# Decayed linear attention and feed-forward: two heads per step on 128 partitions, with zero-padded queries and a 128x128 state

**Chip, cores, metric.** One core of one Trainium2 chip. The metric is the device time of one execution in microseconds (us); medians of several executions are given, with the lowest and highest in brackets.

## The reference

Attention with a decay per head, for B=4 batches, H=8 heads, S=768 tokens, D=64; its result, laid out as x (3072 x 512), goes through a feed-forward part 512 -> 2048 -> 512.

```python
# per head; lam is a scalar per head, near 0.97..0.99
for each block of tokens:
    intra = (qb @ kb.T * Dmask) @ vb              # Dmask[i,j] = lam**(i-j) for i >= j, else 0
    inter = (qb * lam_pow) @ kv_state             # lam_pow[i] = lam**(i+1)
    out[block] = intra + inter
    kv_state = lam_block * kv_state + (kb * rev_pow).T @ vb
...
h = x @ w_in
g = where(h >= 1, h, where(h <= -1, 0, (h + 1)**2 / 4))
return g @ w_out
```

The block length may be chosen freely; both kernels use 128 tokens, so 6 blocks a head.

## The kernel before

q, k and v of two heads are loaded together, q and k scaled on ScalarE into `qkdd` (128 tokens on the partitions, 6 blocks, 4 x 64 columns) and transposed on TensorE. From there each head works by itself on 64 rows or 64 columns of the array.

```python
BLK, GRP = 128, 3
for b in range(B):
    for hp in range(H // 2):
        # ... DMAs of q (L125), k (L128), v (L131); scalings (L137, L140) on ScalarE ...
        qTp = work.tile([128, NCH, 128], BF16, ...)      # two heads: rows 0-63 and 64-127
        kTp = work.tile([128, NCH, 128], BF16, ...)
        # transposes in groups of 4 and 2 into ptr (L152), copies ptr -> qTp, kTp on VectorE (L156)
        for hi in range(2):                              # each head by itself
            ps = hi * 64
            qT, kT = qTp[ps:ps + 64, :, :], kTp[ps:ps + 64, :, :]
            kdd = qkdd[:, :, 2 * D + ps:2 * D + ps + 64]
            for g in range(NG):
                for bi in range(GRP):                    # array form 64*128
                    nc.tensor.matmul(psc[:, bi, :], lhsT=kT[:, blk, :], rhs=qT[:, blk, :], ...)   # L172
                nc.vector.scalar_tensor_tensor(out=sc, in0=psc, scalar=laminvblk[h][:, 0:1],
                                               in1=_bc(causalT, 128, GRP, 128), ...)               # L175
                for bi in range(GRP):
                    nc.tensor.matmul(po[:, bi, :], lhsT=v_bf[:, blk, ps:ps + 64],
                                     rhs=sc[:, bi, :], ...)                        # L183, 128*64
                    if kv is not None:
                        nc.tensor.matmul(po[:, bi, :], lhsT=kv, rhs=qT[:, blk, :], ...)  # L188, 64*64
                    nc.tensor.matmul(pkv[ps:ps + 64, :], lhsT=kdd[:, blk, :],
                                     rhs=v_bf[:, blk, ps:ps + 64], ...)            # L192, 128*64
                    # kv_new = kv * lam**128 + pkv on VectorE (L199 for the first, L202)
                nc.scalar.copy(out=xT[pstart:pstart + 64, ko, ...], in_=po)        # L209
# ... then the feed-forward part, L226 to L252: not touched by the change ...
```

"Array form 64*128" stands for a matmul that contracts over 64 rows and uses 128 columns of the array. The tiles in the profiles: `ptr` holds transposes of q and k, `psc` the scores and `sc` the masked scores, `po` the output of attention, `pkv` what a block adds to the state `kv`; in the feed-forward part, `ph` is the first product and `py` the second.

## Time and profile before

| | before |
|---|---|
| time, median of 4 runs | 387.87 us (387.73 to 388.43) |
| span of the profiled run | 386.0 us |
| end of the last xT copy (end of attention) | 207.1 us |
| rest of the span (feed-forward) | 178.9 us |
| one pair of heads, steady | 10.60 us |

Two rows of the page matter later: the 40 slices of the span (9.65 us each), in tenths busy, and the row of TensorE's granted clock.

### The profile page before, as it was taken

Reading aid. Unit: us, or ns where it says so; the run is one execution under the profiler, and the core shown is the slowest. Engines: PE = TensorE matmul, PEld = TensorE weight load, DVE = VectorE, ACT = ScalarE, POOL = GpSimd, SP = SyncE. Lnnn points to the kernel's source line nnn. Section 1 sums busy time; section 2 is a strip of 40 time slices with the busy share of each in tenths; the row PEclk is TensorE's granted clock in tenths of the full one; section 3 lists DMA queues with packets and bytes.
Section 4 is the critical chain, followed back from the end, with each engine's and each line's share of the span. In section 5 each row is a group of like instructions: output and inputs, shape, how many; then the busy total and the mean of one; then the engine's idle time right before and its main releaser. Section 6 shows DMA issues by size and latency. Waiting matters only on the chain.

```text
span 386.0 us, 5043 instructions
## 1 busy us (share of the span) xinstructions
PE 332.0 (86%) x1680; PEld 161.8 (42%) x1696; DVE 213.3 (55%) x621; ACT 200.9 (52%) x379; POOL 29.5 (8%) x43
## 2 busy tenths in 40 slices
PE   0023899999999999999989999999999999999995
PEld 0012455555555554555543444434434434434432
DVE  1112666666666666666645854834844843852850
ACT  7212333443434433334416966946946955955961
POOL 6000101111111111001100000000000000000000
PEclk9999999999999999999999999999999999999999
DMA  7999977676656655333300011011011011011001
GB/s 154 200 193 192 221 109 102 104 102 99 83 77 77 96 95 93 20 22 21 23 0 0 2 55 54 2 54 55 2 55 54 2 54 54 3 55 55 2 35 75
DMA packets 81482, 26.55 MB, mean 69 GB/s; under 512 B 75824, under 2 KB 77872, under 8 KB 81456
## 3 DMA queue, kind: packets, MB, share of 16 engines
q1 hardware_dynamic: 53776, 18.88, 21.2%
q0 software_dynamic: 27680, 7.34, 18.8%
q8 instruction: 13, 0.21, 0.2%
q14 instruction: 13, 0.11, 0.1%
HBM read 27.27 MB, written 6.29 MB: 87 GB/s over the span
## 4 chain that ended last, share of the span: by engine, by line
PE 60%; DVE 16%; ACT 10%; SPq 5%; issue 4%; DMA 3%; DVEq 0%; ACTq 0%
PE py L246 18%; PE po L183 10%; PE po L188 9%; PE psc L172 7%; PE ptr L152 6%; PE ph L226 6%; DVE a L240 5%; DVE gT L241 5%; ACT cc L235 4%; DMA qk_nat<-in_q_dram 3%; PE pkv L192 3%; DVE aa L238 3%; ACT xT L209 3%; SPq L128 3%; SPq L125 2%
## 5 line engine op out<-in xcount | busy, mean ns | idle before, releaser
L226 PE MATMUL ph<-xT,w_in_sb 128*128 128x512 bf16 x375 | 96.1, 389 | 1.3 <-DVE sc L175 0.2
L246 PE MATMUL py<-w_out_sb,gT 128*128 128x512 bf16 x377 | 92.9, 380 | 2.9 <-DVE gT L241 1.9
L235 ACT ACTIVATE cc<-ph,cm 128x512 bf16<-128x512 f32 x96 | 77.2, 804 | 0.0
L232 ACT ACTIVATE tt<-ph,chalf 128x512 bf16<-128x512 f32 x96 | 76.5, 797 | 1.2 <-PE ph L226 1.2
L209 ACT CAST xT<-po 64x384 bf16<-64x384 f32 x64 | 30.2, 472 | 81.8 <-PE po L188 81.5
L202 DVE SCALAR_TENSOR_TENSOR kv_new<-kv_new,lamblk,pkv 64x64 bf16<-64x64 bf16 x160 | 44.4, 277 | 30.1 <-PE pkv L192 23.2
L226 PEld LDWEIGHTS <-w_in_sb 128*128 128x128 bf16 x384 | 37.7, 98 | 50.7 <-issue 11.3
L246 PEld LDWEIGHTS <-gT 128*128 128x128 bf16 x384 | 35.7, 98 | 52.3 <-DVE gT L241 12.6
L152 PE MATMUL ptr<-ident,qkdd 128*128 128x128 bf16 x192 | 28.8, 307 | 32.3 <-ACT qkdd L137 27.2
L192 PE MATMUL pkv<-v_bf,qkdd 128*64 128x64 bf16 x192 | 49.3, 257 | 8.3 <-DVE kv_new L202 8.3
L238 DVE TENSOR_SCALAR aa<-tt 128x512 bf16<-128x512 bf16 x96 | 27.6, 288 | 51.6 <-ACT tt L232 51.6
L183 PE MATMUL po<-sc,v_bf 128*64 128x128 bf16 x192 | 52.7, 305 | 3.1 <-ACT xT L209 2.5
L175 DVE SCALAR_TENSOR_TENSOR sc<-psc,laminvblk,causalT 128x384 bf16<-128x384 f32 x64 | 39.4, 617 | 25.0 <-PE po L183 9.4
L188 PE MATMUL po<-qTp,kv_new 64*64 64x128 bf16 x160 | 49.8, 312 | 0.6 <-DVE kv_new L202 0.5
L241 DVE TENSOR_TENSOR gT<-a,cc 128x512 bf16<-128x512 bf16 x96 | 40.8, 425 | 10.1
L240 DVE TENSOR_TENSOR a<-aa 128x512 bf16<-128x512 bf16 x96 | 40.8, 425 | 3.3
L252 ACT COPY osb<-py 128x512 f32<-128x512 f32 x24 | 14.0, 586 | 48.2 <-PE py L246 48.2
L137 ACT ACTIVATE qkdd<-qk_nat,lampow_p 128x384 bf16<-128x384 f32 x32 | 19.4, 607 | 36.2 <-PE po L183 27.3
L131 POOL DMA_DIRECT2D v_bf<-in_v_dram x32 | 26.3, 828 | 156.5 <-PE po L188 147.1
L172 PE MATMUL psc<-qTp,kTp 64*128 64x128 bf16 x192 | 36.9, 298 | 1.1 <-DVE kTp L156 0.6
L183 PEld LDWEIGHTS <-v_bf 128*64 128x64 bf16 x192 | 24.7, 132 | 28.4 <-issue 14.1
L152 PEld LDWEIGHTS <-qkdd 128*128 128x128 bf16 x192 | 16.7, 131 | 37.2 <-ACT qkdd L137 27.4
(31 smaller groups left out, 127.1 us busy)
## 6 DMA issues: line engine op xcount, KB each, us to landing
qk_nat<-in_q_dram SPq DMA_DIRECT2D x32, 192.0 KB, 3.6
qk_nat<-in_k_dram SPq DMA_DIRECT2D x32, 192.0 KB, 3.7
out_dram<-osb SPq DMA_DIRECT2D x24, 256.0 KB, 2.0
v_bf<-in_v_dram POOLq DMA_DIRECT2D x32, 96.0 KB, 3.3
w_in_sb<-in_moe_w_in_dram POOLq DMA_DIRECT2D x1, 2048.0 KB, 14.9
w_out_sb<-in_moe_w_out_dram POOLq DMA_DIRECT2D x1, 2048.0 KB, 27.2
lam_b<-in_lam_dram SPq DMA_DIRECT2D x1, 4.0 KB, 2.7
```

The costliest lines, as they stand in the source:

```text
L152: nc.tensor.transpose(out=ptr[:, c, :], in_=qkdd[:, base + c, off:off + 128], identity=ident)
L172: nc.tensor.matmul(psc[:, bi, :], lhsT=kT[:, blk, :], rhs=qT[:, blk, :], start=True, stop=True)
L183: nc.tensor.matmul(po[:, bi, :], lhsT=v_bf[:, blk, ps:ps + 64], rhs=sc[:, bi, :], start=True, stop=(kv is None))
L188: nc.tensor.matmul(po[:, bi, :], lhsT=kv, rhs=qT[:, blk, :], start=False, stop=True)
L192: nc.tensor.matmul(pkv[ps:ps + 64, :], lhsT=kdd[:, blk, :], rhs=v_bf[:, blk, ps:ps + 64], start=True, stop=True)
L202: nc.vector.scalar_tensor_tensor(out=kv_new[ps:ps + 64, :], in0=kv, scalar=lamblk[h][ps:ps + 64, 0:1], in1=pkv[ps:ps + 64, :], op0=AX.mult ...
L226: nc.tensor.matmul(ph, lhsT=w_in_sb[:, ko, ni * 128:(ni + 1) * 128], rhs=xT[:, ko, m0:m0 + MSTRIPE], start=(ko == 0), stop=(ko == KO - 1))
L232: nc.scalar.activation(out=tt, in_=ph, func=AF.Relu, scale=0.5, bias=chalf[:, 0:1])
L235: nc.scalar.activation(out=cc, in_=ph, func=AF.Relu, scale=1.0, bias=cm1[:, 0:1])
L240: nc.vector.tensor_tensor(a2, aa, aa, op=AX.mult)
L241: nc.vector.tensor_tensor(gT[:, ni, :], a2, cc, op=AX.add)
L246: nc.tensor.matmul(py, lhsT=gT[:, ko, msub * 128:(msub + 1) * 128], rhs=w_out_sb[:, ko, :], start=(ko == 0), stop=(ko == FO - 1))
```

## The change

Its intent: work on both heads of a pair at once, so that each matmul fills the 128x128 array and there are fewer of them. q transposed is stored zero-padded (`qTz`: head 0 in rows 0-63 of one half of the columns, head 1 in rows 64-127 of the other), so one matmul of 256 columns gives both heads' scores. The state becomes 128x128 (its cross-head quarters meet only zeros). The decay factor lam^-128 moves from a scalar into the mask, and half of the qTz copies move to ScalarE.

```diff
-    GRP = 3
+    GRP = 2
 # ... exponents of the q and k scalings, kept as columns qsc and ksc; masks pre-multiplied: cut ...
+    for p in range(H // 2):
+        m = const.tile([128, 2, 128], F32, name=f"mask_{p}")
+        lv = const.tile([128, 1], F32, name=f"lamvec_{p}")
+    qTz_bufs = []
+    for j in range(2):
+        t = const.tile([128, NCH, 2, 128], BF16, name=f"qTz_{j}")
+        nc.gpsimd.memset(t, 0.0)
+        qTz_bufs.append(t)
 # ... transposes, now 6 at a time ...
-                        nc.vector.tensor_copy(dst[:, base:base + nchk, :],
-                                              ptr[:, :nchk, :])
+                        if dst is None:
+                            nc.vector.tensor_copy(qTz[0:64, base:base + nchk, 0, :],
+                                                  ptr[0:64, :nchk, :])
+                            nc.scalar.copy(out=qTz[64:128, base:base + nchk, 1, :],
+                                           in_=ptr[64:128, :nchk, :])
+                        else:
+                            nc.vector.tensor_copy(dst[:, base:base + nchk, :],
+                                                  ptr[:, :nchk, :])
-                for hi in range(2):
-                    ... (the per-head loop shown above)
+                for g in range(NG):
+                        nc.tensor.matmul(psc[:, bi, :, :], lhsT=kTp[:, blk, :],
+                                         rhs=qTz[:, blk, :, :], start=True, stop=True)
+                    nc.vector.tensor_tensor(out=sc, in0=psc,
+                                            in1=_ins(masks[hp][:, :, :], 1, GRP), op=AX.mult)
+                        nc.tensor.matmul(po[:, bi, :, :], lhsT=v_bf[:, blk, :],
+                                         rhs=sc[:, bi, :, :], start=True, stop=first)
+                        if not first:
+                            nc.tensor.matmul(po[:, bi, :, :], lhsT=kv,
+                                             rhs=qTz[:, blk, :, :], start=False, stop=True)
+                        nc.tensor.matmul(pkv, lhsT=kddp[:, blk, :],
+                                         rhs=v_bf[:, blk, :], start=True, stop=True)
+                            nc.vector.scalar_tensor_tensor(out=kv_new, in0=kv,
+                                scalar=lamvec[hp][:, 0:1], in1=pkv, op0=AX.mult, op1=AX.add)
+                    for hi in range(2):
+                        nc.scalar.copy(out=xT[ps:ps + 64, hp, mbase:mbase + GRP * 128],
+                                       in_=po[ps:ps + 64, :, hi, :])
```

More of the change, by code (lines that the diff above doesn't have):

```diff
@@ L13, with _ins @@
 AF = mybir.ActivationFunctionType
-def _bc(ap, part, mid, free):
-    a = ap.ap
-    return bass.AP(ap.tensor, ap.offset,
-                   [[a[0][0], part], [0, mid], [a[-1][0], free]])
+def _ins(ap, idx, mid):
+    a = list(ap.ap)
+    a = a[:idx] + [[0, mid]] + a[idx:]
+    return bass.AP(ap.tensor, ap.offset, a)
 @with_exitstack
@@ L58 @@
     nc.scalar.activation(out=ln_lam, in_=lam_b, func=AF.Ln)
-    nln_lam = const.tile([128, H], F32)
-    nc.vector.tensor_scalar_mul(nln_lam, ln_lam, -1.0)
-    iota_p = const.tile([128, 1], I32)
-    nc.gpsimd.iota(iota_p, pattern=[[0, 1]], base=0, channel_multiplier=1)
-    iota_pf = const.tile([128, 1], F32)
-    nc.vector.tensor_copy(iota_pf, iota_p)
+    ep_q = const.tile([128, 1], I32)
+    nc.gpsimd.iota(ep_q, pattern=[[0, 1]], base=0, channel_multiplier=1)
+    ep_k = const.tile([128, 1], I32)
+    nc.gpsimd.iota(ep_k, pattern=[[0, 1]], base=BLK, channel_multiplier=-1)
+    ep_q_f = const.tile([128, 1], F32)
+    nc.vector.tensor_copy(ep_q_f, ep_q)
+    ep_k_f = const.tile([128, 1], F32)
+    nc.vector.tensor_copy(ep_k_f, ep_k)
     c128 = const.tile([128, 1], F32)
@@ L79 @@
     )
-    lampow_p = []
-    revpow_p = []
+    qsc = []
+    ksc = []
     lamblk = []
-    laminvblk = []
     for h in range(H):
-        lp = const.tile([128, 1], F32, name=f"lampow_p_{h}")
-        nc.scalar.activation(out=lp, in_=iota_pf, func=AF.Exp, scale=ln_lam[:, h:h + 1])
-        lampow_p.append(lp)
+        a = const.tile([128, 1], F32, name=f"qsc_{h}")
+        nc.scalar.activation(out=a, in_=ep_q_f, func=AF.Exp, scale=ln_lam[:, h:h + 1])
+        qsc.append(a)
+        b_ = const.tile([128, 1], F32, name=f"ksc_{h}")
+        nc.scalar.activation(out=b_, in_=ep_k_f, func=AF.Exp, scale=ln_lam[:, h:h + 1])
+        ksc.append(b_)
         lb = const.tile([128, 1], F32, name=f"lamblk_{h}")
@@ L91 @@
         lamblk.append(lb)
-        li = const.tile([128, 1], F32, name=f"laminvblk_{h}")
-        nc.scalar.activation(out=li, in_=c128, func=AF.Exp, scale=nln_lam[:, h:h + 1])
-        laminvblk.append(li)
-        r = const.tile([128, 1], F32, name=f"revpow_{h}")
-        nc.scalar.activation(out=r, in_=iota_pf, func=AF.Exp, scale=nln_lam[:, h:h + 1])
-        nc.vector.tensor_single_scalar(r, r, lb[:, 0:1], AX.mult)
-        revpow_p.append(r)
+    c_m128 = const.tile([128, 1], F32)
+    nc.vector.memset(c_m128, -float(BLK))
+    masks = []
+    lamvec = []
+    for p in range(H // 2):
+        m = const.tile([128, 2, 128], F32, name=f"mask_{p}")
+        lv = const.tile([128, 1], F32, name=f"lamvec_{p}")
+        for hi in range(2):
+            h = 2 * p + hi
+            li = const.tile([128, 1], F32, name=f"laminv_{h}")
+            nc.scalar.activation(out=li, in_=c_m128, func=AF.Exp,
+                                 scale=ln_lam[:, h:h + 1])
+            nc.vector.tensor_single_scalar(m[:, hi, :], causalT, li[:, 0:1], AX.mult)
+            nc.vector.tensor_copy(lv[hi * 64:hi * 64 + 64, :],
+                                  lamblk[h][hi * 64:hi * 64 + 64, :])
+        masks.append(m)
+        lamvec.append(lv)
+    qTz_bufs = []
[3 more added lines that the diff above has]
+        qTz_bufs.append(t)
     xT = big.tile([128, KO, n_tok], BF16)
@@ L138 @@
                                   in_=qk_nat[:, :, hi * D:(hi + 1) * D],
-                                  mul=lampow_p[h0 + hi][:, 0:1])
+                                  mul=qsc[h0 + hi][:, 0:1])
                     nc.scalar.mul(out=qkdd[:, :, (2 + hi) * D:(3 + hi) * D],
                                   in_=qk_nat[:, :, (2 + hi) * D:(3 + hi) * D],
-                                  mul=revpow_p[h0 + hi][:, 0:1])
-                qTp = work.tile([128, NCH, 128], BF16, name="qTp", tag="qTp")
+                                  mul=ksc[h0 + hi][:, 0:1])
+                kddp = qkdd[:, :, 2 * D:4 * D]
+                qTz = qTz_bufs[(b * (H // 2) + hp) % 2]
                 kTp = work.tile([128, NCH, 128], BF16, name="kTp", tag="kTp")
-                ei = 0
-                for off, dst in ((0, qTp), (2 * D, kTp)):
-                    for base in range(0, NCH, 4):
-                        nchk = min(4, NCH - base)
-                        ptr = pp_tr.tile([128, 4, 128], BF16, name="ptr", tag="ptr")
+                for off, dst in ((0, None), (2 * D, kTp)):
+                    for base in range(0, NCH, 6):
+                        nchk = min(6, NCH - base)
+                        ptr = pp_tr.tile([128, 6, 128], BF16, name="ptr", tag="ptr")
                         for c in range(nchk):
@@ L155 @@
                                 identity=ident)
-                        nc.vector.tensor_copy(dst[:, base:base + nchk, :],
-                                              ptr[:, :nchk, :])
-                for hi in range(2):
-                    h = h0 + hi
-                    ps = hi * 64
-                    qT = qTp[ps:ps + 64, :, :]
-                    kT = kTp[ps:ps + 64, :, :]
-                    kdd = qkdd[:, :, 2 * D + ps:2 * D + ps + 64]
-                    kv = None
-                    pstart = (h % 2) * 64
-                    ko = h // 2
-                    for g in range(NG):
-                        psc = pp_sc.tile([128, GRP, 128], F32, name="psc", tag="psc")
-                        for bi in range(GRP):
-                            blk = g * GRP + bi
-                            nc.tensor.matmul(psc[:, bi, :], lhsT=kT[:, blk, :],
-                                             rhs=qT[:, blk, :], start=True, stop=True)
-                        sc = scpool.tile([128, GRP, 128], BF16, name="sc", tag="sc")
-                        nc.vector.scalar_tensor_tensor(
-                            out=sc, in0=psc, scalar=laminvblk[h][:, 0:1],
-                            in1=_bc(causalT, 128, GRP, 128),
-                            op0=AX.mult, op1=AX.mult)
-                        po = pp_o.tile([64, GRP, 128], F32, name="po", tag="po")
-                        for bi in range(GRP):
-                            blk = g * GRP + bi
-                            nc.tensor.matmul(po[:, bi, :],
-                                             lhsT=v_bf[:, blk, ps:ps + 64],
-                                             rhs=sc[:, bi, :], start=True,
-                                             stop=(kv is None))
-                            if kv is not None:
-                                nc.tensor.matmul(po[:, bi, :], lhsT=kv,
-                                                 rhs=qT[:, blk, :],
-                                                 start=False, stop=True)
-                            pkv = pp_kv.tile([128, 64], F32, name="pkv", tag="pkv")
-                            nc.tensor.matmul(pkv[ps:ps + 64, :],
-                                             lhsT=kdd[:, blk, :],
-                                             rhs=v_bf[:, blk, ps:ps + 64],
-                                             start=True, stop=True)
-                            kv_new = kvpool.tile([128, 64], BF16,
-                                                 name="kv_new", tag="kv")
-                            if kv is None:
-                                nc.vector.tensor_copy(kv_new[ps:ps + 64, :],
-                                                      pkv[ps:ps + 64, :])
-                            else:
-                                nc.vector.scalar_tensor_tensor(
-                                    out=kv_new[ps:ps + 64, :],
-                                    in0=kv, scalar=lamblk[h][ps:ps + 64, 0:1],
-                                    in1=pkv[ps:ps + 64, :],
-                                    op0=AX.mult, op1=AX.add)
-                            kv = kv_new[ps:ps + 64, :]
-                        mbase = b * S + g * GRP * 128
@@ new lines @@
+                        if dst is None:
+                            nc.vector.tensor_copy(
+                                qTz[0:64, base:base + nchk, 0, :],
+                                ptr[0:64, :nchk, :])
+                            nc.scalar.copy(
+                                out=qTz[64:128, base:base + nchk, 1, :],
+                                in_=ptr[64:128, :nchk, :])
+                        else:
+                            nc.vector.tensor_copy(dst[:, base:base + nchk, :],
+                                                  ptr[:, :nchk, :])
@@ new lines @@
+                kv = None
+                first = True
+                for g in range(NG):
+                    sc = scpool.tile([128, GRP, 2, 128], BF16, name="sc", tag="sc")
+                    psc = pp_sc.tile([128, GRP, 2, 128], F32, name="psc", tag="psc")
+                    for bi in range(GRP):
+                        blk = g * GRP + bi
+                        nc.tensor.matmul(
+                            psc[:, bi, :, :], lhsT=kTp[:, blk, :],
+                            rhs=qTz[:, blk, :, :], start=True, stop=True)
+                    nc.vector.tensor_tensor(
+                        out=sc, in0=psc, in1=_ins(masks[hp][:, :, :], 1, GRP),
+                        op=AX.mult)
+                    po = pp_o.tile([128, GRP, 2, 128], F32, name="po", tag="po")
+                    for bi in range(GRP):
+                        blk = g * GRP + bi
+                        nc.tensor.matmul(
+                            po[:, bi, :, :], lhsT=v_bf[:, blk, :],
+                            rhs=sc[:, bi, :, :], start=True, stop=first)
+                        if not first:
+                            nc.tensor.matmul(
+                                po[:, bi, :, :], lhsT=kv,
+                                rhs=qTz[:, blk, :, :], start=False, stop=True)
+                        pkv = pp_kv.tile([128, 128], F32, name="pkv", tag="pkv")
+                        nc.tensor.matmul(pkv, lhsT=kddp[:, blk, :],
+                                         rhs=v_bf[:, blk, :], start=True, stop=True)
+                        kv_new = kvpool.tile([128, 128], BF16, name="kv_new", tag="kv")
+                        if kv is None:
+                            nc.vector.tensor_copy(kv_new, pkv)
+                        else:
+                            nc.vector.scalar_tensor_tensor(
+                                out=kv_new, in0=kv, scalar=lamvec[hp][:, 0:1],
+                                in1=pkv, op0=AX.mult, op1=AX.add)
+                        kv = kv_new
+                        first = False
+                    mbase = b * S + g * GRP * 128
+                    for hi in range(2):
+                        ps = hi * 64
@@ L209 @@
                         nc.scalar.copy(
-                            out=xT[pstart:pstart + 64, ko, mbase:mbase + GRP * 128],
-                            in_=po)
+                            out=xT[ps:ps + 64, hp, mbase:mbase + GRP * 128],
+                            in_=po[ps:ps + 64, :, hi, :])
     with tc.tile_pool(name="gpool", bufs=2) as gpool, \
```

## The prediction

> **What bounds the kernel now.** I read the page first: the slices (its part 2) show TensorE (PE) near 90% from slice 5 to the end, with the other engines at a half, and its costliest groups name two stages: attention (L152 to L209) and the feed-forward part (L226 to L252), which the diff does not touch. Cut by time, attention's last xT copy ends at 207.1 us of a 386.0 us span, so 178.9 us are feed-forward and stay.
>
> Second, the chain of waits inside attention. Its pieces repeat every 10.60 us, once per pair of heads (16 pairs):
>
> ```profile
> 111.79 0.24 PE po L183
> 112.03 0.05 PE pkv L192
> 112.09 0.24 PE po L188
> 112.33 0.19 PE pkv L192
> 112.52 0.75 PE ptr L152 x6
> ...
> 123.12 0.75 PE ptr L152 x6
> ```
>
> Nearly every piece is PE. The reader is to see that a lone small matmul holds the chain for 0.24 us, but six transposes only 0.75 us.
>
> Third, PE's own timeline in one pair tells what the 0.24 us is:
>
> ```profile
> 82.84 0.31 PE L188 MATMUL po<-qTp,kv_new 64*64 64x128 bf16 x1
> 83.08 0.31 PE L183 MATMUL po<-sc,v_bf 128*64 128x128 bf16 x1
> 83.19 0.26 PE L192 MATMUL pkv<-v_bf,qkdd 128*64 128x64 bf16 x1
> 83.38 0.39 PE L152 MATMUL ptr<-ident,qkdd 128*128 128x128 bf16 x2
> 83.70 0.31 PE L188 MATMUL po<-qTp,kv_new 64*64 64x128 bf16 x1
> 83.95 0.26 PE L192 MATMUL pkv<-v_bf,qkdd 128*64 128x64 bf16 x1
> ```
>
> The second number is each matmul's latency; compare the start times. From L188 (array form 64*64) to L183 (128*64): 0.24 us. From L183 to L192, both 128*64: 0.11. From 128*128 to 64*64: about 0.24. So the form of the array, not the work, sets the pace. A pair has 12 transposes at 128*128, 12 psc at 64*128, 24 po and pkv at 128*64 and 10 po at 64*64 (the groups' counts over 16), in mixed order: 58 matmuls in 10.6 us, 0.183 us each.
>
> Fourth, the groups that the change resizes, and the DMA:
>
> ```profile
> L202 DVE SCALAR_TENSOR_TENSOR kv_new<-kv_new,lamblk,pkv 64x64 bf16<-64x64 bf16 x160 | 44.4, 277 | 30.1 <-PE pkv L192 23.2
> L175 DVE SCALAR_TENSOR_TENSOR sc<-psc,laminvblk,causalT 128x384 bf16<-128x384 f32 x64 | 39.4, 617 | 25.0 <-PE po L183 9.4
> L209 ACT CAST xT<-po 64x384 bf16<-64x384 f32 x64 | 30.2, 472 | 81.8 <-PE po L188 81.5
> L137 ACT ACTIVATE qkdd<-qk_nat,lampow_p 128x384 bf16<-128x384 f32 x32 | 19.4, 607 | 36.2 <-PE po L183 27.3
> ```
>
> VectorE (DVE) and ScalarE (ACT) have idle time in front of all of them, so they are followers. The stretches give DMA share 1.38 and 202 GB/s in 30 to 50 us (saturated), but 0.69 and 98 GB/s in 80 to 90 us.
>
> [...] N=512 starts are 0.216 us apart, transposes about 0.107. [...] Here L137-type work of 0.61 us starts every 0.52 us[...].
>
> **The change part by part.** Two heads share the 128 partitions: the zero-padded qTz makes psc and po one 128*128 matmul of 256 columns for both heads, and kv a 128x128 state. The built order of instructions shows 35 matmuls a pair, all 128*128: no mode change is left.
>
> TensorE per pair: 12 transposes and 6 pkv at 0.107 = 1.93; 6 psc and 11 po at 0.109 = 1.85; together 3.8 us instead of 10.6. TensorE stops being the bound.
>
> VectorE per pair: 3 sc of 512 columns[...]; 5 kv updates of 128 columns[...]; first kv[...]; two copies of 768 columns. From the old copies, 425 ns at 512 columns and about 280 at 256, the slope is 0.56 ns, so 570 each (1.14). Sum 5.4 us, some 4.8 with overlap. Before: 4x617 + 10x277 + 2x222 + 1413 (copies) = 7.1.
>
> ScalarE per pair: 4 scalings of 0.61; six xT copies of 64x256[...]; one new qTz copy of 64x768[...]. Sum 5.4 us, some 4.5 with overlap (before 4.3).
>
> So no engine needs more than 5 us, and the pair's loop of dependences sets the pace. I walked the built order by hand with these durations and about 50 ns per semaphore hop (the trace's sc follows its psc by that). From the first psc of a pair: two psc ready 0.45, [...] then PE streams its queue (po, pkv5, transposes of the next pair, po3) and starts the last pkv at 3.9, done 4.2. That pkv frees the qkdd buffer, for which ScalarE waits: one scaling (0.52), then, behind it in its order, the qTz copy[...], then the next pair's psc. [...] A second loop, through the kTp copy on VectorE, comes to 5.4. I take 5.7 us a pair.
>
> Start and end. The opening is bound by DMA (weights beside q and k): before, the first po runs at 38.1 us, when pair 1's inputs have come, and the new order waits for the same. Pairs 0 and 1 then run together, pair 0 done at about 42.4. v of pair 2 can only then be fetched (two buffers): 1.65 us of issue and 3.3 us of landing, so pair 2 starts at about 47.8. Thirteen steps of 5.7 make 121.9 for pair 15; 4.2 to its last po[...] give 127.2. Plus 178.9 is a span of 306, plus the 1.9 by which the time exceeds the span: 308 us. The setup (masks, zeroing of qTz, new exponents) lies in the time that waits for data and costs nothing on the path.
>
> **The rivals.** (a) DMA becomes the bound. A pair's 3,072 packets of q and k and 1,536 of v fill 0.69 of the share for 10.6 us; at the saturated 1.38 that is 5.3 us. This lies so close below 5.7 that contention may lengthen v's landing. v's own loop has about 1.8 us of slack in two periods; if landing goes from 3.3 to 6 us a pair takes 6.3 and the time is 316. For: the saturated start; against: q and k are fetched four pairs ahead. (b) ScalarE or VectorE dearer than estimated (the strided, half-partition qTz copies)[...]: each makes the period 6.3 to 7, the time 316 to 326. (c) The zero padding doubles the multiply work and cancels the gain, so about 380: would need TensorE to have been bound by streaming columns; the 0.24 us at mode changes speaks against it. (d) ScalarE runs further ahead than I assumed and the loop closes at 5.0: 299 us.
>
> **Range and chances.** Thirteen steps of 5.0 to 7.0 us a pair span 299 to 325; I give 297 to 326 around 308. Only (c), or a breakage that I do not see, would leave it within 2%. Faster 0.97, same 0.02, slower 0.01.
>
> **What would show it.** Right: all PE attention groups 128*128; starts of po L204 and psc L194 about 0.11 us apart when nothing waits; a repeat of 5 to 6.5 us; last xT near 127 us and feed-forward again near 179; PE share in attention at 60 to 75%. Idle before PE should name ACT qTz and DVE sc. Wrong: a repeat of 7 us or more; DMA share at 1.3 with PE waiting for v_bf; feed-forward longer than 179.

The sums came to 5.4 us a pair on VectorE, 5.4 on ScalarE, 5.6 for the loop, taken as 5.7, and 127.2 for the last xT copy, which led to 308 us. The 0.109 us for 256 columns: half of the 0.216 for 512 is 0.108, and the kernel after shows 0.108 to 0.109 at full clock. The overlap on VectorE is in the trace of the kernel before: its durations add up to the 7.1 us, and it is busy 17.34 of 27 us, which is 6.8 a pair. Of the hop of about 50 ns the trace shows 38, from the end of the last psc to the start of sc. "Saturated" is an inference from one stretch: with four v buffers the share was 1.61 in 60 to 70 us, at 200 GB/s. "Mode" stands for the array form.

## More of the kernel before

```profile
PE   0023899999999999999989999999999999999995
PEclk9999999999999999999999999999999999999999
```

TensorE looks busy and at full clock in the whole of attention (slices 5 to 21).

## The result, and the profile after

| | before | after |
|---|---|---|
| time, median | 388.31 us (387.73 to 388.65, 13 runs) | 310.26 us (309.07 to 311.84, 9 runs) |
| ratio, fast runs | | 0.7995, 95% interval 0.7978 to 0.8011 |
| span of the profiled run | 386.0 us | 308.9 us |
| end of the last xT copy | 207.1 us | 127.1 us |
| rest of the span | 178.9 us | 181.8 us |
| one pair of heads, steady | 10.60 us | 5.47 us |

A ratio is the mean time of one kernel's fast runs over that of the other's of the same rounds, so it is not quite the ratio of the medians quoted. Here and below it is over the kernel before.

Attention ended 80.0 us sooner and the rest took 2.9 us longer: 77.1 us of span. The same rows of the page, for the kernel after (a slice is 7.7 us), with ScalarE's (ACT):

```profile
PE   0102467677676776998999999989999999999993
ACT  7701167899999988898279719962995399349930
PEclk9999995999999989999999999999999999999999
```

In slices 7 to 16 TensorE is down to six or seven tenths, and ScalarE is at nine in slices 9 to 14. The clock row has a 5, in slice 7: it is a hint of something that the row of the kernel before did not show.

TensorE's timeline within one pair of the kernel after (start in us, latency in us, line, tile, array form, columns):

```profile
91.38 0.27 PE L204 MATMUL po<-sc,v_bf 128*128 128x256 bf16 x1
91.49 0.27 PE L208 MATMUL po<-qTz,kv_new 128*128 128x256 bf16 x1
91.60 0.27 PE L204 MATMUL po<-sc,v_bf 128*128 128x256 bf16 x1
91.70 0.27 PE L208 MATMUL po<-qTz,kv_new 128*128 128x256 bf16 x1
91.81 0.22 PE L212 MATMUL pkv<-v_bf,qkdd 128*128 128x128 bf16 x1
91.87 0.55 PE L171 MATMUL ptr<-ident,qkdd 128*128 128x128 bf16 x7
```

One form throughout, and starts 0.11 us apart where before it was 0.19 to 0.25 at a change (medians by the two lines; 0.242 from po L188 to po L183). A 128-column matmul (L212) lets the next one start after 0.06 us.

The groups that answer to those in the prediction (line, engine, operation, tiles and count, then total busy time and mean ns of one, then idle time ahead of them and what ended most of it):

```profile
L197 DVE TENSOR_TENSOR sc<-psc,mask 128x512 bf16<-128x512 f32 x48 | 31.7, 685 | 20.7 <-PE psc L194 19.8
L227 ACT CAST xT<-po 64x256 bf16<-64x256 f32 x96 | 35.2, 367 | 8.3 <-PE po L208 6.8
L218 DVE SCALAR_TENSOR_TENSOR kv_new<-kv_new,lamvec,pkv 128x128 bf16<-128x128 bf16 x80 | 27.2, 341 | 4.2 <-PE pkv L212 1.4
L194 PE MATMUL psc<-qTz,kTp 128*128 128x256 bf16 x96 | 17.7, 297 | 6.7 <-ACT qTz L179 6.5
```

The xT copies are the same work as before in half-as-wide pieces (30.2 us before, 35.2 now), but their idle time fell from 81.8 to 8.3 us: ScalarE no longer waits for TensorE. TensorE's psc waits for ScalarE's qTz copy instead.

Busy time of the engines in one steady pair and in a long stretch of attention (stretch, its length, then PE, PEld (TensorE's weight loads), DVE, ACT, POOL busy, granted clock, DMA share, GB/s). First the kernel before:

```profile
73.00:100.00 27.00, 25.11 (x149) 13.98 (x148) 17.34 (x50) 9.68 (x19) 3.56 (x5) 1.00 0.61 96
```

And the kernel after:

```profile
73.00:100.00 27.00, 18.29 (x173) 13.43 (x172) 23.15 (x54) 25.84 (x55) 7.82 (x11) 1.00 1.25 178
89.39:94.86 5.47, 3.71 (x35) 2.73 (x35) 4.72 (x12) 5.23 (x12) 1.64 (x3) 1.00 1.16 157
```

TensorE went from 93% busy to 68%; ScalarE from 36% to 96%. In the one pair ScalarE works 5.23 of 5.47 us. Its timeline there:

```profile
89.36 0.74 ACT L227 CAST xT<-po 64x256 bf16<-64x256 f32 x2
90.14 0.61 ACT L159 ACTIVATE qkdd<-qk_nat,ksc 128x384 bf16<-128x384 f32 x1
90.66 0.60 ACT L156 ACTIVATE qkdd<-qk_nat,qsc 128x384 bf16<-128x384 f32 x1
91.16 0.60 ACT L159 ACTIVATE qkdd<-qk_nat,ksc 128x384 bf16<-128x384 f32 x1
91.79 1.51 ACT L227 CAST xT<-po 64x256 bf16<-64x256 f32 x4
93.38 0.61 ACT L156 ACTIVATE qkdd<-qk_nat,qsc 128x384 bf16<-128x384 f32 x1
94.02 0.79 ACT L179 COPY qTz<-ptr 64x768 bf16<-64x768 bf16 x1
```

There is no gap worth naming. The scalings start about 0.51 us apart though each takes 0.61, so they overlap; the xT copies take 0.37 each, and four take 1.51: they do not overlap.

### The profile page after: what moved, and what is told of

It reads as the page before. It is cut to its first block, busy times and chain, and to the rows that moved or that the text cites. A ratio compares the mean times of both kernels' runs of the same rounds, so it can differ in the third digit from the quotient of the medians.

```text
span 308.9 us, 4117 instructions
## 1 busy us (share of the span) xinstructions
PE 240.9 (78%) x1312; PEld 121.7 (39%) x1328; DVE 180.9 (59%) x486; ACT 218.1 (71%) x427; POOL 32.1 (10%) x46
## 4 chain that ended last, share of the span: by engine, by line
PE 24%; DVE 19%; ACT 14%; issue 5%; DVEq 0%; ACTq 0%
PE py L263 21%; ACT cc L252 7%; DVE a L257 7%; DVE gT L258 7%; ACT tt L249 4%; DVE aa L255 4%; PE ph L243 2%; ACT xT L227 1%; PE ptr L171 1%; ACT qkdd L156 1%; PE po L204 1%; ACT qTz L179 1%; PE po L208 0%; ACT qkdd L159 0%; DVE kTp L183 0%
## 5 line engine op out<-in xcount | busy, mean ns | idle before, releaser
L243 PE MATMUL ph<-xT,w_in_sb 128*128 128x512 bf16 x376 | 90.6, 378 | 1.3
L197 DVE TENSOR_TENSOR sc<-psc,mask 128x512 bf16<-128x512 f32 x48 | 31.7, 685 | 20.7 <-PE psc L194 19.8
L227 ACT CAST xT<-po 64x256 bf16<-64x256 f32 x96 | 35.2, 367 | 8.3 <-PE po L208 6.8
L204 PE MATMUL po<-sc,v_bf 128*128 128x256 bf16 x96 | 25.3, 299 | 9.5 <-DVE sc L197 6.1
L218 DVE SCALAR_TENSOR_TENSOR kv_new<-kv_new,lamvec,pkv 128x128 bf16<-128x128 bf16 x80 | 27.2, 341 | 4.2 <-PE pkv L212 1.4
L159 ACT ACTIVATE qkdd<-qk_nat,ksc 128x384 bf16<-128x384 f32 x32 | 19.4, 607 | 12.4 <-DMA qk_nat<-in_k_dram 12.0
L212 PE MATMUL pkv<-v_bf,qkdd 128*128 128x128 bf16 x96 | 19.7, 235 | 10.5 <-DMA v_bf<-in_v_dram 5.3
L156 ACT ACTIVATE qkdd<-qk_nat,qsc 128x384 bf16<-128x384 f32 x32 | 19.4, 607 | 9.0 <-DMA qk_nat<-in_q_dram 4.5
L208 PE MATMUL po<-qTz,kv_new 128*128 128x256 bf16 x80 | 23.3, 300 | 0.1
L194 PE MATMUL psc<-qTz,kTp 128*128 128x256 bf16 x96 | 17.7, 297 | 6.7 <-ACT qTz L179 6.5
```

Source lines behind the costliest of these rows:

```text
L197: nc.vector.tensor_tensor(out=sc, in0=psc, in1=_ins(masks[hp][:, :, :], 1, GRP), op=AX.mult)
L204: nc.tensor.matmul(po[:, bi, :, :], lhsT=v_bf[:, blk, :], rhs=sc[:, bi, :, :], start=True, stop=first)
L218: nc.vector.scalar_tensor_tensor(out=kv_new, in0=kv, scalar=lamvec[hp][:, 0:1], in1=pkv, op0=AX.mult, op1=AX.add)
L227: nc.scalar.copy(out=xT[ps:ps + 64, hp, mbase:mbase + GRP * 128], in_=po[ps:ps + 64, :, hi, :])
L243: nc.tensor.matmul(ph, lhsT=w_in_sb[:, ko, ni * 128:(ni + 1) * 128], rhs=xT[:, ko, m0:m0 + MSTRIPE], start=(ko == 0), stop=(ko == KO - 1))
```

## The experiments

Two questions: what made TensorE slow before, and what sets the pace after. For the first, the theory was the changes of array form (call it F); the rival was the count of matmuls and the work per head. A second rival appeared on reading the traces together and is told under "the clock".

**1. One form, and nothing else.** The kernel before, still head by head with its 58 matmuls a pair and its groups of 3, but each padded to 128*128. (It needs zeroed buffers for q and the state, and ScalarE does half of the qTz copies, as in the change.)

```diff
-                    qT = qTp[ps:ps + 64, :, :]
-                    kT = kTp[ps:ps + 64, :, :]
-                    kdd = qkdd[:, :, 2 * D + ps:2 * D + ps + 64]
+                    qT = qTz[:, :, hi, :]
+                    kT = kTp
+                    kdd = qkdd[:, :, 2 * D:4 * D]
-                                             lhsT=v_bf[:, blk, ps:ps + 64],
+                                             lhsT=v_bf[:, blk, :],
-                            kv_new = kvpool.tile([128, 64], BF16, ...)
+                            kv_new = kvz_bufs[nkv % 2]        # 128x128, zeroed once
```

> The kernel before, one head at a time as before (58 matmuls a pair, 10 kv updates of 64 columns a pair on VectorE), but every matmul padded to 128*128, so that none of the 32 changes of form a pair is left; one new half copy for q goes to ScalarE. Theory F (changes of form set the pace of attention, and TensorE is held at half clock with them): same-form starts at 0.06 to 0.11 us, VectorE's 7.1 us a pair becomes the bound, a pair takes 7.2 to 8.5 us instead of 10.6, time 340 to 360 us. Rival P (the pairing of heads, that is fewer matmuls and half the serial kv steps, made the gain): 375 us or more. Rival C (the low clock is not tied to the changes of form): transposes keep the 314 ns latency; with theory F they fall to about 219.

Measured: 341.25 us (339.99 to 341.76), ratio 0.8775 (0.8754 to 0.8797). The last xT copy ends at 160.7 us; a pair takes 7.8 us. So 47 of the 78 us come with the one form alone, though the padding doubles or quadruples the products that TensorE forms. The other 31 are what is left for the rest of the change (two heads at once, with its new groups and masks), which was not taken apart further. The time is as F forecast, but the transposes are not all at the 219 ns that went with it: they take 216 to 314 ns with 311 as median, and the granted clock in attention went up and down (means of 0.67 to 0.84 in the windows of 10 us from 60 to 150 us). So this run alone does not say by which means the one form helps, which led to the next question.

**The clock.** The matmul that transposes a 128x128 block is the same instruction in every kernel here, so its latency is a gauge of the clock. The view of one tile gives minimum, median and maximum in ns. In the kernel before:

```profile
L152 PE MATMUL ptr<-ident,qkdd x192: 265/314/314, 21.6 to 189.5; 128*128 128x128 bf16 x192
```

In the kernel after, and in experiment 1:

```profile
L171 PE MATMUL ptr<-ident,qkdd x192: 217/219/314, 12.6 to 121.4; 128*128 128x128 bf16 x192
```

```profile
L163 PE MATMUL ptr<-ident,qkdd x192: 216/311/314, 12.6 to 148.1; 128*128 128x128 bf16 x192
```

Where the kernel after has a recorded clock of one half (one such stretch):

```profile
45.20:55.40 10.20, 8.44 (x54) 6.18 (x53) 6.03 (x14) 7.15 (x17) 1.77 (x3) 0.50 1.51 202
```

its transposes take 287 to 314 ns, with 311 as median; where the clock is full (55.4 to 113.4 us), 217 to 230, with 219 as median. The kernel before has 314 as median and never less than 265. The ends of matmuls are modelled, as the page's legend says, so compare the starts too, and they agree: transposes that follow each other start 0.107 us apart in the kernel after at half clock and 0.056 at full clock, and 0.106 us apart in the kernel before (median of 146). So **TensorE ran at half clock through practically all of attention in the kernel before**. The row of nines is an artefact: that trace's first clock record starts at 210.0 us, and the page fills what comes before it as full (it gives 1.00 for 73 to 100 us, where transposes take 314 ns). From 210 us on, in the feed-forward part, the clock is full in both.

A new rival, then: the gain is the clock's (call it C). Experiments 2 to 4 look for F and C one at a time.

**2. A change of form at full clock.** The kernel after, with a useless 64-column matmul after every second py matmul of the feed-forward part, where the clock is full: once in the form 128*128 (the control), once in 64*64.

```diff
+                    if ko % 2 == 1:
+                        pd = pp_d.tile([128, 64], F32, name="pd", tag="pd")
+                        nc.tensor.matmul(pd, lhsT=ident[:, :], rhs=ident[:, 0:64], ...)            # control
+                        nc.tensor.matmul(pd[0:64, :], lhsT=ident[0:64, 0:64],
+                                         rhs=ident[0:64, 0:64], ...)                               # tiled
```

> The kernel after, with 192 useless matmuls of 64 columns put between the second feed-forward matmuls, where TensorE runs at full clock without pause; same 128*128 form. Control for the next run. Expected: each costs 0.03 to 0.06 us of streaming, in all +6 to +12 us on 310.

> As the run before, but the 192 small matmuls are 64*64, so that each brings two changes of form at full clock. If a change costs[...], the starts of neighbours are 0.15 to 0.35 us further apart and the time is 50 to 70 us over that of the control. If a change is free at full clock, and the 0.24 us before came from the half clock alone, the time equals the control's within 3 us.

Measured: control 316.24 us (314.05 to 316.92), ratio 0.8131 (0.81 to 0.8162); tiled 346.99 us (345.37 to 349.74), ratio 0.894 (0.8896 to 0.8983). TensorE's timeline in the control:

```profile
150.20 0.19 PE L271 MATMUL pd<-ident 128*128 128x64 bf16 x1
150.23 0.60 PE L264 MATMUL py<-w_out_sb,gT 128*128 128x512 bf16 x2
150.66 0.19 PE L271 MATMUL pd<-ident 128*128 128x64 bf16 x1
```

and in the tiled one:

```profile
150.02 0.60 PE L264 MATMUL py<-w_out_sb,gT 128*128 128x512 bf16 x2
150.56 0.21 PE L271 MATMUL pd<-ident 64*64 64x64 bf16 x1
150.70 0.61 PE L264 MATMUL py<-w_out_sb,gT 128*128 128x512 bf16 x2
151.24 0.21 PE L271 MATMUL pd<-ident 64*64 64x64 bf16 x1
```

In the control the next matmul starts 0.03 us after a small one, the low end of what was expected. From small matmul to small matmul it is 0.46 us in the control and 0.68 in the tiled kernel. That is 0.22 us for two changes, **0.11 us for each change of form at full clock**. The time rose by 30.75 us for 192 small matmuls, 0.16 each and not 0.22, presumably since some of it lies beside other waits; the expectation put it at 50 to 70 us, so the size was overestimated. F is real and does not need the half clock: a change costs at full clock too. In the kernel before it was 0.24 us from start to start, where the same form goes on after 0.107; about 0.135 us extra, at half clock.

**3. Useless columns into the kernel before.** If the clock follows the columns streamed, more useless streaming should bring it up. One useless matmul of 448 columns ahead of each pkv, in pkv's own form (so that no change of form is added), and then three of them.

```diff
+                            pkv = pp_kv.tile([128, 512], F32, name="pkv", tag="pkv")
+                            nc.tensor.matmul(pkv[ps:ps + 64, 64:512], lhsT=kdd[:, blk, :],
+                                             rhs=w_in_sb[:, 0, 0:448], ...)      # once, or three times
-                            nc.tensor.matmul(pkv[ps:ps + 64, :],
+                            nc.tensor.matmul(pkv[ps:ps + 64, 0:64],
```

> The kernel before with one useless matmul of 448 columns ahead of each pkv, in pkv's own form and into unused columns of its bank: 12 more a pair, no further change of form. It makes the array stream more columns between the changes. If low activity is why the granted clock is half in attention, the fillers raise it: transposes' latency 219 ns instead of 314, a change of form costs some 0.15 instead of 0.24, so a pair takes 10.6 - 32 x 0.09 + 12 x 0.19 = 10.0 us, time about 378. If the clock stays at half whatever the activity, a pair takes 10.6 + 12 x 0.375 = 15.1 us, time about 455.

> As e2 (before, fillers in pkv's 128*64 form), but three fillers a pkv. The columns streamed are then some 79% of the half-clock cycles, more than e1's 68% where the clock flipped, but only half of the array works, about 41% by area. If the clock follows the columns streamed, it rises: transposes 219 ns, time about 440. If it follows the area (or the tiled forms as such), it stays at half: transposes 314 ns, time about 590.

(The times of a filler in these two fit the traces: 0.19 us for 448 columns is 448/512 of the 0.216 us between starts of 512 columns in the feed-forward part, and 0.375 is 448/128 of the 0.107 us between transposes. The 79% are an estimate from them: 6,656 + 36 x 448 columns in 10.6 + 36 x 0.375 = 24.1 us. The 0.15 us for a change was an estimate; 0.170 was measured, below.)

Measured: one filler 440.19 us (440.06 to 440.61), ratio 1.1333 (1.1317 to 1.135); three fillers 427.45 us, one run only. The gauge with one filler:

```profile
L152 PE MATMUL ptr<-ident,qkdd x192: 286/314/314, 22.2 to 237.7; 128*128 128x128 bf16 x192
```

and with three:

```profile
L152 PE MATMUL ptr<-ident,qkdd x192: 219/219/314, 19.9 to 230.7; 128*128 128x128 bf16 x192
```

One filler (12 a pair) was not enough: the clock stayed at half and the kernel only grew longer, a pair taking 13.9 us. Of the two expectations it is the half clock that came, if at 440 us and not 455. Three (36 a pair) brought the clock to full from 39.3 us on, and three times as much useless work took 12.7 us less than one time as much (13.05 us a pair). With the clock full, a change from po to po costs 0.170 us from start to start where it was 0.242. So the low clock is a second cause, and here it rose when many more columns were streamed. It does not follow the rate of form changes: the kernel with one filler has 32 in 13.9 us and stayed at half, the one with three has them in 13.05 us and went up. What the clock follows stays open: of the columns that a half clock could stream (128 in each 0.107 us), the kernel before uses an estimated 52% (6,656 columns in the 10.60 us of a pair) and the kernel with one filler 72% (12,032 in 13.9), and both stayed at half; experiment 1 uses an estimated 71% (6,656 in 7.8) and went up and down; three fillers would at half clock use the 79% of their expectation, and went up.

**4. Useless columns into experiment 1.** The same there, with a 448-column matmul in the one form.

```diff
+                            pkv = pp_kv.tile([128, 512], F32, name="pkv", tag="pkv")
+                            nc.tensor.matmul(pkv[:, 64:512], lhsT=kdd[:, blk, :],
+                                             rhs=w_in_sb[:, 0, 0:448], start=True, stop=True)
```

> The run e1 (one head at a time, one form) with a useless 128*128 matmul of 448 columns ahead of each pkv. [...] If the clock follows how much of the array works, it stays full in attention now, transposes take 219 ns, and although TensorE has 12 more matmuls a pair (2.3 us at full clock) the time stays at 341 or falls to 330. If not, the fillers cost 12 x 0.37 us a pair and the time is 365 or more.

Measured: 337.60 us (336.2 to 338.27), ratio 0.8686 (0.8666 to 0.8707). The gauge and the stretch that was read above:

```profile
L163 PE MATMUL ptr<-ident,qkdd x192: 215/219/315, 12.6 to 147.1; 128*128 128x128 bf16 x192
```

```profile
73.00:100.00 27.00, 23.93 (x251) 15.15 (x251) 24.21 (x73) 18.14 (x36) 6.58 (x8) 1.00 0.90 125
```

Full clock, 12 useless matmuls a pair more, and still 1% faster than experiment 1. VectorE is now busy 24.21 of 27 us (90%), and TensorE with its fillers 23.93 (89%). In experiment 1, without fillers, VectorE was busy 23.48 us of the same stretch and TensorE 21.18. So at one form, head by head, VectorE is the fullest engine, at 7.47 us a pair with the clock full; that it is the bound is likely, but no run relieved it alone. The second half of the change (fewer, wider VectorE instructions) lightens it.

**5. A few changes of form put back.** The kernel after, with each pkv as two matmuls of 64 weight columns; 8 changes of form a pair, as the order of the matmuls in the trace shows, against 32 in the kernel before.

```diff
-                        nc.tensor.matmul(pkv, lhsT=kddp[:, blk, :],
-                                         rhs=v_bf[:, blk, :], start=True, stop=True)
+                        for hi in range(2):
+                            nc.tensor.matmul(pkv[hi * 64:hi * 64 + 64, :],
+                                lhsT=kddp[:, blk, hi * 64:hi * 64 + 64],
+                                rhs=v_bf[:, blk, :], start=True, stop=True)
```

> The kernel after with each pkv split again into two matmuls of 64 columns of weights (form 128*64): 6 more matmuls and 8 changes of form a pair, the rest as after. A change at full clock measured 0.11 us on the run with the small tiled matmuls. In the kernel after TensorE was busy 3.7 of a pair's 5.47 us and ScalarE 5.23. If the changes only fill TensorE's slack, the time stays within 1% of 310; if they lie on the way from psc to the last pkv, for which ScalarE's scaling waits, a pair takes 0.3 to 0.9 us longer and the time is 314 to 322; if they bring the half clock back, 325 or more and transposes of 314 ns.

Measured: 323.44 us (318.02 to 327.61), ratio of the two fast runs of four 0.823 (0.8188 to 0.8273), against 0.7995 for the kernel after. In the profiled run, which is one of the two slow ones, the gauge is 314 ns as median and 229 at the least, the granted clock has a mean of 0.937 over the span, and a pair takes 6.83 us. The fast runs have no profile, and their mean granted clock over the span (0.967 and 0.951) is at the low end of that of the kernel after (0.963 to 0.994) or under it, so the part that the clock takes in their loss is not shown.

**6. What paces the kernel after.** The prediction had a loop of dependences (L): the last pkv frees a qkdd buffer, then scaling, then the qTz copy, then psc. The rival (S): ScalarE is simply full. A third qkdd buffer cuts L; moving one scaling to VectorE relieves S.

```diff
-                qkdd = work.tile([128, NCH, 4 * D], BF16, name="qkdd", tag="qkdd")
+                qkdd = work.tile([128, NCH, 4 * D], BF16, name="qkdd", tag="qkdd", bufs=3)
```

> The kernel after with a third qkdd buffer, so that ScalarE's scaling no longer waits for the last pkv of the pair before. The prediction named the loop through that wait as the pace (5.6 us). Theory L (that loop): a pair falls to 5.3 us or less, time 306 to 308. Theory S (ScalarE itself is full: 5.23 us busy of each 5.47): the time stays within 1% of the kernel after and ScalarE's busy share stays at 95% or more.

Measured: 311.76 us (310.21 to 312.74), ratio 0.8024 (0.8001 to 0.8048): no gain. The clock fell more often in the profiled run (means of 0.83, 0.87, 0.96 and 0.83 in the four windows of 10 us from 80 to 120 us; the kernel after has one stretch of 3.4 us at half, from 113.4 us on), so the pair at full clock is the better test: 5.4 us, against 5.47 with two buffers and the 5.3 or less that L asked for. In 60 to 80 us, at full clock, ScalarE is busy 19.00 of 20 us, with two buffers 19.11:

```profile
60.00:80.00 20.00, 12.35 (x127) 9.45 (x125) 16.58 (x42) 19.00 (x42) 6.44 (x8) 1.00 1.38 195
```

L is not the pace.

```diff
-                    nc.scalar.mul(out=qkdd[:, :, (2 + hi) * D:(3 + hi) * D],
-                                  in_=qk_nat[:, :, (2 + hi) * D:(3 + hi) * D],
-                                  mul=ksc[h0 + hi][:, 0:1])
+                    if hi == 0:
+                        ...                       # as before
+                    else:
+                        nc.vector.tensor_scalar_mul(qkdd[:, :, (2 + hi) * D:(3 + hi) * D],
+                            qk_nat[:, :, (2 + hi) * D:(3 + hi) * D], ksc[h0 + hi][:, 0:1])
```

> The kernel after with one of ScalarE's four scalings a pair moved to VectorE (0.52 us of ScalarE's 5.23 us a pair; VectorE had 4.63[...]). Theory S (ScalarE is full and sets the pace of the new attention): a pair falls from 5.47 to 5.0 to 5.2 us, time 304 to 308. Rival: the chain of dependences through TensorE and VectorE sets it, then the time stays at 310 or rises, as VectorE's kv updates come later.

Measured: ratio of fast runs 0.7932 (0.7904 to 0.7959); median 309.67 us (306.36 to 314.62, two of six runs slow). A pair takes 5.22 us where the clock is full, but 6.5 where it fell (mean 0.72 in 88 to 100 us), and one pair took 6.5 at full clock, since TensorE waited 2.2 us for v. S holds: a pair falls by 0.25 us. That is half of the 0.52 taken from ScalarE, so the next limit is near (the scaling that VectorE got takes it 0.46 us, as measured in the run of all three below; the estimate of it in the expectation is cut); in 60 to 66 us VectorE is as full as ScalarE (5.54 and 5.50 of 6 us). The clock may be one limit more: its mean over the four fast runs is 0.973, over the ten runs of the kernel after 0.981. That it falls because TensorE gets emptier is not shown.

**7. Useful uses of this.** First, keep the clock up with a useless 384-column matmul ahead of each pkv of the kernel after; then four v buffers, for the wait for v.

```diff
-                        pkv = pp_kv.tile([128, 128], F32, name="pkv", tag="pkv")
-                        nc.tensor.matmul(pkv, lhsT=kddp[:, blk, :],
+                        pkv = pp_kv.tile([128, 512], F32, name="pkv", tag="pkv")
+                        nc.tensor.matmul(pkv[:, 128:512], lhsT=kddp[:, blk, :],
+                                         rhs=w_in_sb[:, 0, 0:384], start=True, stop=True)
+                        nc.tensor.matmul(pkv[:, 0:128], lhsT=kddp[:, blk, :],
```

> The kernel after with a useless matmul of 384 columns ahead of each pkv (6 a pair, 1.0 us of TensorE at full clock; TensorE had 1.8 us to spare). If columns streamed hold the clock, it is full from the first bodies on and through the stretches at 45 to 55 and 113 to 117 us where the kernel after fell to half; the spread of its runs (309.1 to 311.8) shrinks and the time is 306 to 310. If TensorE's spare time was needed, 312 or more.

```diff
-                v_bf = work.tile([128, NCH, 2 * D], BF16, name="v_bf", tag="v_bf")
+                v_bf = work.tile([128, NCH, 2 * D], BF16, name="v_bf", tag="v_bf", bufs=4)
```

> The kernel after with four v_bf buffers instead of two, so that v of pair 2 is fetched ahead and not only when pair 0 is done. The prediction put pair 2's start at 47.8 us because of that wait. If it is real, pair 2's first pkv starts earlier than the 49.1 us of the kernel after and the time falls by 2 to 6 us, to 304 to 308. If the opening is bound by bandwidth anyway (the share is at 1.36 to 1.5 there), v only takes it from q and k and the time stays within 1 us of 310.

Measured: filler 306.04 us (305.3 to 307.69), ratio 0.789 (0.7872 to 0.7908), 1.3% under the kernel after by the ratios, with the clock full from 40.4 us on and the last xT copy at 123.6. The gain lies before pair 3, in the stretch that ran at half clock in the kernel after: pair 3's psc starts at 53.2 us instead of 56.5, and the 12 steps from there to pair 15 take 65.7 us, where they took 65.8. Four v buffers 307.88 us (305.57 to 312.81, one of five runs slow), ratio 0.791 (0.789 to 0.793); pair 2's transposes begin at 43.9 us instead of 44.9, its first pkv at 46.7 instead of 49.1, and TensorE waits for v no more. With the filler, what TensorE waits for is v (waiting engine and line, what for, total us, times, longest):

```profile
PE pkv L214 <- DMA v_bf<-in_v_dram: 8.7, 9, 1.6
```

The last run took all three together (one scaling on VectorE, filler, four v buffers).

> The three edits to the kernel after that each gave something, together: one scaling on VectorE (5.22 us a pair where the clock was full), the 384-column fillers that hold the clock, four v_bf buffers. If the gains add, a pair takes 5.0 to 5.2 us and pair 2 starts 1 to 2 us earlier: time 300 to 304. If the transfers (at 1.5 to 1.6 of the share in the last runs; 983 KB a pair at 200 GB/s is 4.9 us) have become the bound, it stays at 304 to 306 and TensorE or ScalarE wait for q, k or v.

Measured: 308.31 us (307.93 to 308.88), ratio 0.7941 (0.793 to 0.7952), so the gains do not add, and neither forecast came: it is not q, k or v that TensorE waits for. A pair takes 5.63 us with the clock full, and psc waits for the scaling that VectorE now does, behind its other work:

```profile
PE psc L200 <- DVE qkdd L164: 5.7, 11, 0.5
```

The fastest kernel is the kernel after with the filler alone. Filler and four v buffers without the scaling on VectorE, which this result points to, were not run.

## Why the prediction was right, and where by luck

The direction, the amount and the mechanism's main step hold: 308 predicted, 310.26 measured. Point by point:

- **The form of the array sets TensorE's pace: right, but half the story.** Experiment 1 gives 47 of 78 us for one form alone, and experiment 2 prices a change by itself. Missed was that TensorE ran at half clock in the kernel before. The prediction measured 0.24 us a change in the trace, so the clock was inside its number without being seen. How the 47 us divide between the changes themselves and the clock is not settled: fewer changes also let more columns through in the same time, and the clock rose with more columns when fillers were added (gauge 314 ns with one, 219 with three). An estimate of a ceiling: with three fillers at full clock a pair takes 13.05 us, of which 36 x 0.189 = 6.8 are fillers (448/512 of the 0.216 us between starts of 512 columns; the trace has fillers 0.19 us apart), so TensorE would need some 6.3 us instead of 10.6. VectorE, with 7.1 us of work by the prediction's sum (6.7 us busy in the 7.47 of experiment 4's pair), would bind first. By this estimate the kernel before, with all its changes of form, would at full clock come to about where experiment 1 is (7.8 us a pair), so the clock may be worth most of the 47 us; no run shows it.
- **TensorE 3.8 us a pair: right by two errors.** Measured 3.71 busy. The prediction took the 0.107 us between transposes from the kernel before, where TensorE ran at half clock; in the kernel after they start 0.107 us apart at half clock, but at full clock transposes and pkv start 0.056 us apart. That leaves 18 x 0.056 + 17 x 0.109 = 2.9 us of issue; the 3.71 counts latencies too. A gap read in a stretch whose clock is not known should not be carried to another.
- **VectorE and ScalarE rows.** sc takes 685 ns, the kv update 341, the first kv 291 to 293, the qTz copies 550 on VectorE (570 predicted) and 794 on ScalarE, the xT copy 367. But for that 570, the predicted times of these are cut: they rested on rates per element that no trace then showed. What the two traces show is not one rate: the kv update grew by 64 ns for 64 columns (1.0 ns each), sc by 68 ns for 128 (0.53 each; its instruction also changed, from SCALAR_TENSOR_TENSOR to TENSOR_TENSOR), and the xT copy fell by 105 ns for 128 (0.82 each). VectorE is busy 4.72 us (4.8 predicted).
- **The pace.** This is the step that failed in kind. Predicted: a loop of 5.6 us, taken as 5.7, with ScalarE at 4.5 us. Measured: 5.47 us, and ScalarE at 5.23 of them. The mis-sized term is the overlap of ScalarE's six xT copies: the prediction took it from the scalings, which do overlap, and the copies do not (0.378 us apart for 367 ns of work). That the copies read PSUM does not explain it by itself: the feed-forward's ACTIVATEs read PSUM too and overlap (797 ns and more each, 570 apart). Its undiscounted sum, 5.4 us, was there in the same paragraph. With ScalarE full, the third buffer of experiment 6 gains next to nothing (5.4 us a pair).
- **Start and end.** Pair 2's psc came at 49.3 us (predicted 47.8). The wait for v is as predicted, but longer: v was issued from 42.3 us on, and TensorE, which stood idle for it at the end, could use it at 49.1, after 6.9 us and not 1.65 + 3.3. The 13 steps from pair 2 to pair 15 took 73.0 us (74.1 predicted), a mean of 5.6 that meets the predicted 5.7 by luck: 5.47 when steady, with 7.2 and 6.4 where the clock fell. The tail took 4.8 us (5.3 predicted), so the errors cancelled and the last xT copy ended at 127.12 (127.2). The rest took 181.8 us, not 178.9, which the prediction itself had named a sign of being wrong. (Its 1.9 us from span to time also took two different runs; in the profiled run it is 387.73 - 386.0 = 1.7.) Before, 10 matmuls of the feed-forward part ran ahead of the last xT copy, after, 6: about 0.9 us (4 x 0.216); the other 2.0 were not followed up.
- **Rivals.** (c), padding cancels the gain, is refuted by experiment 1. (a), v's landing, shows as a side limit: 4.1 us of waits in 60 to 110 us, 8.7 in 50 to 120 once the clock is full (the sign that the prediction named for it, PE waiting for v at a DMA share of 1.3, came in part: the share is 1.25 in 73 to 100 us). (b), dearer engines, did not come. Nor did (d), ScalarE ahead and 5.0 us a pair: with the third buffer, which lets it run ahead, a pair takes 5.4.

## What to carry to other kernels

Before believing a row that says full clock, measure one known matmul in the stretch (the transposes of 128 columns here: 219 ns at full, 311 to 314 at half as medians, and starts 0.056 and 0.107 us apart), and compare it with the same matmul in a stretch known to be at full clock. Keep one array form in a stream of small matmuls, even if zero padding multiplies the products (here 388 to 341 us), and if TensorE then has room, useless columns may pay by holding the clock up (here 310 to 306 us). When adding up an engine's time, give an overlap only to those instructions whose start times show it.
